# 100 small fill-ups and two large ones first, one product on VectorE, one group of transposes moved forward

## The chip, the cores and the metric

The kernel runs on one core of one Trainium2 chip. The metric is the device time of one execution in microseconds (us). The kernel before took 466.82 us, the median of three runs (466.12 to 467.25).

The engines are TensorE (PE in the profile; its weight loads are a stream of their own, PEld), VectorE (DVE), ScalarE (ACT), GpSimd (POOL) and SyncE (SP), which here issues the transfers.

## The reference

A gated linear attention over four batches, eight heads, 768 steps and a head size of 48, and behind it a two-layer block on 3072 tokens.

```python
f = 1.0 / (1.0 + np.exp(-f_logit))
for t in range(S):
    state = f[:, :, t, :, None] * state + np.einsum('bhd,bhe->bhde', k[:, :, t], v[:, :, t])
    y[:, :, t] = np.einsum('bhd,bhde->bhe', q[:, :, t], state)
x = y.transpose(0, 2, 1, 3).reshape(B * S, H * D)
h = x @ w_in                                  # 384 -> 2048
g = h * np.clip(h + 3.0, 0.0, 6.0) / 6.0
return g @ w_out                              # 2048 -> 384
```

## The kernel before

The attention is cut into 24 units, one for each batch and chunk of 128 steps; unit `i` has batch `i % 4` and chunk `i // 4`, so units 0 to 3 are the first chunks of the four batches. The two-layer block is cut into six groups of 512 tokens (the four units of one chunk) by 16 slices of 128 hidden columns.

The order of all work is written out by hand in `ORDER` (L55): a list of tokens such as `kv.1.2`, which means step `kv` of unit 1 with PSUM bank 2. The tokens are issued one after the other, and each engine executes its own instructions strictly in the order of the list (the loop at the end of `gla_moe` chains them). So a token's place relative to another one matters only where both have instructions on one engine. `ON_POOL` (L48) lists the elementwise steps that go to GpSimd instead of VectorE; the function `engine` looks them up.

What the early tokens do, with the lines under which the profile shows them:

- `load`, `loadq`, `loadv`, `ld`, `hole`: transfers on SP (gates, q and k, v, a slice of the weights in float32, and rows of the attention's output that are moved between partitions).
- `gate` (ScalarE, L321): sigmoid. `back` (VectorE, L327) and `fwd` (L347): scans over the gates, backwards and forwards. `rend` (VectorE, L343 and L344): the ends of the decay and their reciprocals.
- `kmul` (L340) and `qmul` (L353): k and q times the decay. `kmul.1` stands in `ON_POOL` and runs on GpSimd; the other early ones run on VectorE.
- `tk` (TensorE, L411): four transposes of k. `ktok` (ScalarE, L418): their copy out of PSUM.
- `kv` (TensorE, L430): the state's update, 24 matmuls in a unit of the first chunk; every float32 matmul is two passes in the profile, so 48. `carry0`, `carry1` (ScalarE, L443 and L450, in the first chunk): its copies out of PSUM.
- `att` (TensorE, L392) and `mask` (VectorE, L399): the scores inside a chunk. `qs` (TensorE, L461) and `av` (L478): the two parts of the output, "values" in what follows.
- `xh` (ScalarE, L497), `xs` (TensorE, L501), `xl` (ScalarE, L508): the output split into a high and a low half-precision part.
- `z` (ScalarE, L243), `cy` (ScalarE, L252), `mid` (VectorE, L256), `dif` (L263), `top` (L267), `high` (ScalarE, L272), `lowi` (L275): the rounding and splitting of a slice of weights.
- `mm1a`, `relua`, `ga`, `mm2a` and their kin: the two-layer block.
- `warm.n` (L804): a fill-up. It multiplies the zero tile `blank` into the bank `idle`, which nothing reads, in matmuls of up to four times 128 columns: `warm.16` is four matmuls of 512 columns, `warm.3` one of 384. Being float32, each is two passes. TensorE executes them in its order like any other matmul.

At the start VectorE clears `blank`, and TensorE begins with `warm.16`. `tk.0` waits for `kmul.0`, `ktok.0` for `tk.0`, `kv.0` for `ktok.0`, `att.0` for `carry0.0` (it takes over the PSUM bank) and `qmul.0`, `mask.0` for `att.0`, and `av.0` for `mask.0` and `qs.0`.

## Time and profile before

| | us |
|---|---|
| median of three runs | 466.82 |
| lowest and highest run | 466.12, 467.25 |
| the profiled execution | 468.3 |
| its span, first to last instruction | 466.6 |

The profile's page gives the busy time of each engine with its share of the span and its number of instructions, the chain of work that ended last with its shares, and the groups of instructions. Times in the trace are counted from the start of the span. A row of the timeline reads: start, duration in us, engine, line, operation, output and input tiles, shape, number of instructions merged, and in brackets the idle time of the engine before it with what ended it ("issue" where the profile names nothing). A row of the windows view reads: the stretch, its length, then busy time and number of instructions of PE, PEld, DVE, ACT and POOL, the granted TensorE clock as a share of full speed, the busy share of the DMA engines, and GB/s. In the DMA view, a line gives a queue with its kind, packets, MB and share of 16 engines. Some matmul records can be missing from a trace, a few per cent.

### The profile page before, as it was taken

How to read it: one execution, taken by the hardware profiler on the slowest of the kernel's cores; microseconds unless marked ns; L12 is line 12 of the kernel's file. 1: busy time of each engine (PE TensorE's matmuls, PEld its weight loads, DVE VectorE, ACT ScalarE, POOL GpSimd, SP SyncE). 2: the span in 40 equal slices, each digit the busy share in tenths (PEclk: the TensorE clock that was granted, in tenths of full speed). 3: DMA queues.
4: the chain of work that ended last, by engine and by line, in shares of the span. 5: the costliest groups of instructions: out<-in, count | busy, mean ns of one | idle time of the engine just before them, and what ended most of it. 6: DMA issues, size and time to landing. Idle time of an engine off the chain costs nothing.

```text
span 466.6 us, 11487 instructions
## 1 busy us (share of the span) xinstructions
PE 459.2 (98%) x4963; PEld 247.5 (53%) x4963; DVE 300.1 (64%) x508; ACT 205.1 (44%) x344; POOL 79.3 (17%) x85
## 2 busy tenths in 40 slices
PE   8899999999999999999999999999999999999996
PEld 4678855544445644554545444665644444555543
DVE  6889999968697748746443596879752312423554
ACT  3577777764353243435142541344433423233332
POOL 3000311132012320322210051241200231000000
PEclk9799999999999999999999999999999999999999
DMA  8569647520430150510212120522020000010002
GB/s 301 188 249 353 249 181 249 198 84 0 135 108 1 51 206 0 153 46 0 87 31 91 42 94 1 196 90 76 4 80 0 1 0 6 24 45 3 0 1 68
DMA packets 25396, 43.09 MB, mean 92 GB/s; under 512 B 2560, under 2 KB 17152, under 8 KB 25344
## 3 DMA queue, kind: packets, MB, share of 16 engines
q1 hardware_dynamic: 23744, 41.56, 26.0%
q8 instruction: 39, 0.64, 0.6%
q10 hardware_dynamic: 1600, 0.79, 0.6%
q14 instruction: 13, 0.11, 0.1%
HBM read 36.43 MB, written 4.72 MB: 88 GB/s over the span
## 4 chain that ended last, share of the span: by engine, by line
PE 97%; DVE 1%; ACT 1%; issue 1%; DVEq 0%
PE o L582 35%; PE pair L536 26%; PE single L536 13%; PE pair L461 3%; PE o L621 3%; PE pair L478 3%; PE pair L392 3%; PE pair L430 2%; PE idle L804 2%; PE o L593 2%; PE pair L636 1%; PE single L636 1%; PE single L603 1%; PE pair L603 1%; PE pair L411 1%; PE single L411 1%
## 5 line engine op out<-in xcount | busy, mean ns | idle before, releaser
L582 PE MATMUL o<-gg,weight 128*128 128x512 f16 x744 | 170.2, 379 | 0.0
L536 PEld LDWEIGHTS <-weight 128*128 128x128 f16 x819 | 78.7, 98 | 93.6 <-issue 0.8
L536 PE MATMUL pair<-xts,weight 128*128 128x512 f16 x549 | 125.9, 379 | 0.0
L582 PEld LDWEIGHTS <-weight 128*128 128x128 f16 x744 | 72.0, 98 | 82.4 <-issue 0.7
L555 ACT ACTIVATE gg<-tg 128x512 f16<-128x512 f32 x88 | 54.5, 627 | 62.5 <-DVE tg L550 56.1
L550 DVE SCALAR_TENSOR_TENSOR tg<-tg,pair 128x512 f32<-128x512 f32 x61 | 41.3, 682 | 62.7 <-ACT tg L546 62.6
L546 ACT ACTIVATE tg<-pair,half 128x512 f32<-128x512 f32 x61 | 41.5, 683 | 66.6 <-PE pair L536 64.8
L565 POOL TENSOR_TENSOR gg<-tg,gg 128x512 f16<-128x512 f32 x33 | 40.1, 1225 | 167.1 <-ACT gg L555 148.1
L536 PE MATMUL single<-xts,weight 128*128 128x512 f16 x270 | 63.3, 379 | 0.0
L550 DVE SCALAR_TENSOR_TENSOR tg<-tg,single 128x512 f32<-128x512 f32 x30 | 20.5, 683 | 33.2 <-ACT tg L546 33.2
L546 ACT ACTIVATE tg<-single,half 128x512 f32<-128x512 f32 x30 | 20.6, 686 | 45.0 <-PE single L536 43.3
L347 DVE TENSOR_TENSOR_SCAN suffix<-gates,rend 112x516 f32<-112x516 f32 x24 | 30.6, 1276 | 4.3 <-POOL qkf L340 3.7
L327 DVE TENSOR_TENSOR_SCAN suffix<-gates,unit 112x516 f32<-112x516 f32 x24 | 29.9, 1248 | 5.1 <-ACT gates L321 5.0
L565 DVE TENSOR_TENSOR gg<-tg,gg 128x512 f16<-128x512 f32 x39 | 27.0, 702 | 8.4 <-ACT gg L555 8.2
L497 ACT ACTIVATE xts<-pair 112x512 f16<-112x512 f32 x24 | 14.3, 595 | 30.2 <-PE pair L478 17.8
L340 POOL TENSOR_TENSOR qkf<-qkf,suffix 112x512 f32<-112x512 f32 x13 | 17.0, 1309 | 47.1 <-DVE suffix L327 43.4
L399 DVE TENSOR_TENSOR a<-pair,causal 128x512 f32<-128x512 f32 x24 | 16.4, 684 | 13.0 <-PE pair L392 10.2
L510 DVE SCALAR_TENSOR_TENSOR xts<-pair,xts 112x512 f16<-112x512 f32 x20 | 13.6, 682 | 8.5 <-ACT xts L497 8.4
L321 ACT ACTIVATE gates<-gates 112x512 f32<-112x512 f32 x24 | 14.9, 623 | 5.2 <-DMA gates<-fg 5.2
L430 PE MATMUL pair<-v,ktok 64*48 64x48 f32 (+1 forms) x768 | 15.8, 214 | 1.3 <-issue 1.3
L478 PE MATMUL pair<-a,v 64*48 64x64 f32 (+1 forms) x768 | 16.2, 222 | 0.6 <-DVE a L399 0.2
L392 PE MATMUL pair<-qkf 48*64 48x64 f32 x768 | 16.4, 224 | 0.2 <-ACT state L450 0.2
(99 smaller groups left out, 447.5 us busy)
## 6 DMA issues: line engine op xcount, KB each, us to landing
qkf<-qk SPq DMA_DIRECT2D x24, 512.0 KB, 5.0
raw<-w SPq DMA_DIRECT2D x16, 768.0 KB, 5.6
gates<-fg SPq DMA_DIRECT2D x24, 258.5 KB, 3.7
v<-v SPq DMA_DIRECT2D x24, 200.0 KB, 3.3
outT<-os SPq DMA_DIRECT2D x10, 256.0 KB, 2.7
outT<-os SPq DMA_DIRECT2D x10, 128.0 KB, 1.9
xts<-xts SPq DMA_DIRECT2D x48, 24.0 KB, 1.9
outT<-os ACTq DMA_DIRECT2D x2, 256.0 KB, 2.6
```

The source lines that it names most:

```text
L327: nc.vector.tensor_tensor_scan(flat(sf)[:, ::-1], gt[:, 1:][:, ::-1], flat(unit)[:, ::-1], 0.0, op0=ALU.mult, op1=ALU.add,)
L340: engine("kmul", i).tensor_tensor(parts_of(t, 1), parts_of(t, 1), split(sf[:, :, 1:C + 1]), op=ALU.mult)
L347: nc.vector.tensor_tensor_scan(flat(sf), gt[:, :NP * (C + 1)], flat(rend), 0.0, op0=ALU.mult, op1=ALU.add,)
L392: nc.tensor.matmul(d["at"][HC * odd:HC * (odd + 1), e, 2 * n + c], t[rs, 1, n, c, odd], t[rs, 0, n, c, odd], start=True, stop=True,)
L430: nc.tensor.matmul(d["kv"][r:r + m, odd, c, n], d["ktok"][rs, 2 * n + part, r:r + m], heads_of(vt[rs], part, n, e)[:, :D], start=(odd, e) ...
L478: nc.tensor.matmul(d["y"][to:to + m, odd, n, cs], heads_of(vt[rs], c, n, e)[:, :m], d["a"][rs, 2 * n + c, e], start=False, stop=True, skip ...
L536: nc.tensor.matmul(h, win[:, f, a, k * 128:(k + 1) * 128], g["xt"][:, k, :g["n"] // C, b], start=i == 0, stop=i == 3 * KT - 1,)
L546: nc.scalar.activation(d["t"], d["h"], AF.Relu, bias=half, scale=RISE)
L550: nc.vector.scalar_tensor_tensor(d["t"], d["t"], TOP, d["h"], op0=ALU.min, op1=ALU.mult)
L555: nc.scalar.activation(d["gg"][:, 0], d["t"], AF.Copy)
L565: engine("gl", int(g["name"]) * NF + f).tensor_tensor(d["gg"][:, 1], d["t"], d["gg"][:, 0], op=ALU.subtract)
L582: nc.tensor.matmul(g["o"][m], wout[:, f, a, m * 128:(m + 1) * 128], g[f]["gg"][:, b], start=f == 0 and i == 0, stop=f == NF - 1 and i == 2 ...
```

## The change

Four things are edited.

1. `warm.16` at the start becomes `brief.100 warm.8`. `brief.100` is a new token: 100 matmuls of a bf16 zero tile `small` with 32 weight columns and 32 moving columns, into a corner of `idle`. `warm.8` is two matmuls of 512 columns. The tile `small` is cleared on VectorE ahead of `blank`.
2. `kmul.1` leaves `ON_POOL`, so it runs on VectorE, and its token moves to a place ahead of `rend.1`.
3. `tk.1.4 ktok.1` moves ahead of `av.0 xh.0`.
4. The fill-up `warm.1` ahead of `av.0` is dropped.

```diff
 ON_POOL = """
-kmul.1 decay.4 kmul.6 lowi.5 kmul.7 decay.7 lowi.7 kmul.8 gl.9 decay.8 gl.11 qmul.8 gl.12 lowo.0 low.15 lowo.3 gl.19
+decay.4 kmul.6 lowi.5 kmul.7 decay.7 lowi.7 kmul.8 gl.9 decay.8 gl.11 qmul.8 gl.12 lowo.0 low.15 lowo.3 gl.19
...
 ORDER = """
-load.0 gate.0 back.0 loadq.0 loadv.0 rend.0 kmul.0 load.1 fwd.0 gate.1 back.1 warm.16 tk.0.3 ktok.0 warm.4 kv.0.0
-carry0.0 load.2 qmul.0 warm.1 att.0.0 loadq.1 ld.0 rend.1 qs.0.2 mask.0 gate.2 warm.1 av.0 xh.0 kmul.1 tk.1.4 ktok.1
+load.0 gate.0 back.0 loadq.0 loadv.0 rend.0 kmul.0 load.1 fwd.0 gate.1 back.1 brief.100 warm.8 tk.0.3 ktok.0 warm.4 kv.0.0
+carry0.0 load.2 qmul.0 warm.1 att.0.0 loadq.1 ld.0 kmul.1 rend.1 qs.0.2 mask.0 gate.2 tk.1.4 ktok.1 av.0 xh.0
 carry1.0 fwd.1 qmul.1 warm.3 att.1.0 xs.0 loadv.1 back.2 mask.1 rend.2 cy.0 load.3 kv.1.2 z.0 mid.0 loadq.2 gate.3
...
+    small = const.tile([128, 64], BF16, name="small")
+    nc.vector.memset(small, 0.0)
     blank = const.tile([128, 128], F32, name="blank")
     nc.vector.memset(blank, 0.0)
...
-        if op == "warm":
+        if op == "brief":
+            for _ in range(i):
+                nc.tensor.matmul(idle[:32, :32], small[:, :32], small[:, :32], start=True, stop=True)
+        elif op == "warm":
             for at in range(0, i, 4):
```

The early stretch of `ORDER` that the prediction follows, behind these lines, is the same in both:

```python
carry1.0 fwd.1 qmul.1 warm.3 att.1.0 xs.0 loadv.1 back.2 mask.1 rend.2 cy.0 load.3 kv.1.2 z.0 mid.0 loadq.2 gate.3
back.3 ld.1 carry0.1 warm.1 qs.1.0 dif.0 kmul.2 top.0 fwd.2 xl.0 carry1.1 loadq.3 av.1 hole.0 tk.2.4 rend.3 xh.1 xs.1
xl.1 z.1 qmul.2 warm.3 att.2.2 kmul.3 cy.1 mid.1 fwd.3 ktok.2 loadv.2 high.0 warm.4 kv.2.0 carry0.2 tk.3.4 ktok.3
```

## The prediction

> **What bounds the kernel now.** I read the page's busy times and the chain of work that ended last, then the list of what each engine waited for, split at 30 us, then the timeline, the DMA view and the one-microsecond windows of the first 30 us.

> ```profile
> PE 459.2 (98%) x4963; PEld 247.5 (53%) x4963; DVE 300.1 (64%) x508; ACT 205.1 (44%) x344; POOL 79.3 (17%) x85
> q8 instruction: 39, 0.64, 0.6%
> PE 97%; DVE 1%; ACT 1%; issue 1%; DVEq 0%
> ```

> TensorE is the bound: 97% of the chain. Asked for 30 to 467 us, the waits view lists no wait of TensorE at all. So a microsecond gained or lost before 30 us moves the end by about a microsecond: every transfer and every other engine behind it waits for a buffer or a result that moves along. The change lies wholly before 30 us.

> ```profile
> PE pair L430 <- issue: 1.3, 1, 1.3
> DVE raw L256 <- ACT top L252: 2.0, 1, 2.0
> 14.70 0.78 PE L430 MATMUL pair<-v,ktok 64*64 64x48 f32 x34
> 16.75 0.66 PE L430 MATMUL pair<-v,ktok 64*48 64x48 f32 x14 [1.27 <-issue]
> 0.00:15.47 15.47, 13.88 (x220) 7.93 (x221) 11.63 (x23) 7.22 (x13) 4.23 (x17) 1.00 0.88 328
> q1 hardware_dynamic: 1556, 4.52, 87.4%
> q8 instruction: 1, 0.02, 4.6%
> q8 instruction: 1, 0.02, 3.8%
> ```

> The one large hole of TensorE is the 1.27 us in the middle of `kv.1`: 34 of its 48 matmuls run, then nothing, and no semaphore is named. The last three lines are the DMA view of 0 to 14 us, where the data queue is the only one, and the instruction queue's line of 14.0 to 15.4 and of 17.5 to 19.0 us: one packet each, and none between. The page has 39 such packets for 2 x 4963 TensorE instructions, 254 each. So I read the hole as a lack of instructions: 220 + 221 = 441 were there at the start, the next block came in near 15 us, and TensorE went on at 16.75. One block earlier is instruction 441 - 254 = 187; TensorE passes it inside `att.0`, near 10.4 us. If the request goes out there, 6.3 us pass until use, while the data queue keeps the DMA engines full.

> ```profile
> 16.00:17.00 1.00, 0.25 (x12) 0.25 (x12) 1.00 (x2) 0.00 (x0) 0.00 (x0) 0.90 0.08 33
> 18.00:19.00 1.00, 0.91 (x21) 0.67 (x24) 1.00 (x3) 0.50 (x2) 0.00 (x0) 0.50 0.00 0
> 23.00:24.00 1.00, 1.00 (x29) 0.82 (x22) 0.39 (x2) 1.00 (x3) 0.00 (x0) 0.69 0.14 38
> ```

> The third number from the right is the granted clock, the next the DMA share. The clock is 1.00 in the stretch to 15.47, then 0.90, 0.50 and 0.69: halved from about 16.8 to 23.6 us, right after the hole.

> **The change part by part.** *The fill-ups.* Before, `warm.16` is four instructions, eight passes, and `tk.0` stands behind them.

> ```profile
> 1.13 6.38 PE L804 MATMUL idle<-blank 128*128 128x512 f32 x8 [1.13 <-DVE blank L208]
> 7.34 0.55 PE L411 MATMUL pair<-ident,qkf 112*128 112x112 f32 x4
> 7.73 1.04 PE L804 MATMUL idle<-blank 128*128 128x512 f32 x2
> 22.58 1.13 PE L392 MATMUL pair<-qkf 48*64 48x64 f32 x32
> ```

> The first eight passes start some 0.8 us apart, the pair at 7.73 us needs 0.52 each: the first run at half clock. Four of them go, 3.4 us, and 100 small matmuls come. No row shows one of 32 by 32. The nearest is the last one above: at half clock, 32 matmuls of 64 columns in two-pass f32, on four parts of the array in turn, take 1.13 us, 0.035 each. On one part that is at most 0.14 a matmul, and a quarter of that, 0.035, for half the columns in one pass of bf16. The lower end is 0.027, by the last row less its run-out of some 0.25 us ((1.13 - 0.25) / 32). The upper end is 0.054, twice that, if no weight load hides behind the matmul before it; but loads (247.5 us) do run beside matmuls (459.2 us) in a span of 466.6. I take 0.035: 3.5 us, for 3.4 removed. The ends are 2.7 and 5.4 us, that is `tk.0` 0.7 us earlier or 2.0 later. Earlier brings at most 0.35 us, since `ktok.0` stands behind `gate.1` on ScalarE. The memset of the small tile costs under 0.1 us on VectorE ahead of `blank`, at a time when VectorE then waits for the first gates anyway.

> *Where the instruction blocks fall.* The small ones add 100 pairs, four passes fewer take 4, the fill-up `warm.1` ahead of `av.0` takes 2: 94 pairs, 188 instructions more. Instruction 187 now falls among the small ones, near 4.3 us, and instruction 442 in the first third of `av.0`, near 11.8 us. The same 6.3 us from request to use gives 10.6 us: in time by 1.2. The block behind that starts at 441 + 254 = 695, in `av.1`; it is requested at 11.8, the data queue is nearly empty by 16 us (share 0.08), and I let it be usable at 16.75 as before, when `av.1` is just due. So both waits are about zero, and 1.27 goes.

> *`kmul.1` on VectorE.*

> ```profile
> 8.97 1.48 POOL L340 TENSOR_TENSOR qkf<-qkf,suffix 112x512 f32<-112x512 f32 x1 [5.24 <-DVE suffix L327]
> 9.32 1.16 DVE L343 TENSOR_SCALAR ends<-suffix 112x4 f32<-112x4 f32 x1
> 15.15 0.16 DVE L343 TENSOR_SCALAR ends<-suffix 112x4 f32<-112x4 f32 x1
> 10.89 0.69 DVE L399 TENSOR_TENSOR a<-pair,causal 128x512 f32<-128x512 f32 x1 [0.20 <-PE pair L392]
> 17.43 0.68 DVE L340 TENSOR_TENSOR qkf<-qkf,suffix 112x512 f32<-112x512 f32 x1
> ```

> GpSimd needs 1.48 us, and the `ends` operation beside it takes 1.16 instead of 0.16. After, the product takes 0.68 on VectorE (last row) and `ends` 0.16 again: 0.32 us less ahead of `mask.0`. That buys nothing: `mask.0` already waits 0.20 for `att.0`, and its wait grows to about 0.5. On GpSimd, `decay.4` is next, a later unit's. SP's queue keeps its order; no DMA is added or moved.

> *`tk.1`, `ktok.1` in front of `av.0`, `xh.0`.*

> ```profile
> 10.58 0.41 PE L461 MATMUL pair<-qkf,middle 48*64 48x64 f32 x16
> 11.64 0.69 PE L478 MATMUL pair<-a,v 64*64 64x64 f32 x32 [0.23 <-DVE a L399]
> 12.76 0.69 DVE L353 TENSOR_TENSOR qkf<-qkf,suffix 112x512 f32<-112x512 f32 x1
> 12.90 0.54 ACT L418 ACTIVATE ktok<-single 128x448 f32<-128x448 f32 x1
> 13.34 0.33 ACT L450 ACTIVATE state<-pair 112x192 f32<-112x192 f32 x1
> 13.71 0.69 PE L392 MATMUL pair<-qkf 48*64 48x64 f32 x32 [0.19 <-ACT state L450]
> 14.34 0.43 PE L501 MATMUL pair<-xts,less 112*112 112x256 f16 x2
> 17.68 0.59 ACT L508 ACTIVATE xts<-pair 112x512 f16<-112x512 f32 x1
> ```

> `tk.1` (0.55, as `tk.0`) takes the place of the removed fill-up, about 11.0 to 11.55 us, while `mask.0` runs until 11.58. Behind it wait `av.0`, then `xh.0` and `carry1.0` on ScalarE. `kmul.1` is done by 10.1, so the new wait is empty; were it late, `av.0` would be late by as much. `ktok.1` (0.54) moves out from between `xh.0` and `carry1.0`, so the latter starts near 13.0 instead of 13.34. `att.1` (13.71) then waits for `qmul.1`, which VectorE ends at 13.45, and comes 0.1 us earlier. VectorE, busy without a gap to 21.61, takes no notice: counted as 0.

> *What follows when the hole is gone.*

> ```profile
> 15.18 0.61 ACT L321 ACTIVATE gates<-gates 112x512 f32<-112x512 f32 x1
> 18.85 1.13 PE L478 MATMUL pair<-a,v 64*64 64x64 f32 x32
> 20.92 0.69 DVE L340 TENSOR_TENSOR qkf<-qkf,suffix 112x512 f32<-112x512 f32 x1
> 21.91 0.88 ACT L243 ACTIVATE whole<-raw 128x768 int32<-128x768 uint32 x1
> 22.69 0.89 ACT L252 ACTIVATE top<-raw 128x768 int16<-128x768 int16 x1
> 23.61 0.36 DVE L256 TENSOR_SCALAR raw<-top 128x768 int16<-128x768 int16 x1 [2.00 <-ACT top L252]
> 24.70 0.91 PE L430 MATMUL pair<-v,ktok 64*64 64x48 f32 x48
> ```

> `kv.1` runs through: 14.70 + 0.91 = 15.6. ScalarE is free from `gate.3` at 15.79, so `carry0.1` (0.33) ends at 16.15, `qs.1` (0.41) at 16.6, `av.1` (0.69 at full clock) at 17.35 instead of 19.98. Now `tk.2` is late next: it waits for VectorE's `kmul.2` (17.43 + 0.68 = 18.11) and ends at 18.8; `xs.1` (0.43) 19.2, `xl.1` (0.59) 19.8, then `z.1` and `cy.1` on ScalarE, 0.88 and 0.89: 21.6. VectorE comes free at 21.61. So `mid.1` starts at 21.65 instead of 23.61: **2.0 us**. On TensorE `kv.2` follows the fill-up behind `att.2`: VectorE's `qmul.2`, just ahead of the row at 20.92, is done by 21.0; `att.2` 0.69 and `warm.4` 1.04 later it is 22.7 instead of 24.70, 2.0 too. The sum is 0 + 0 + 0 + 2.0.

> The profiled execution took 468.3 us with a span of 466.6; the median of the three timed runs is 466.82. I take the 2.0 from the median: **464.8 us**. With the fill-ups at their short end it is 464.4.

> [...] The clock fell behind a hole of 1.27 us, the longest TensorE had. [...]

> **The rivals.** *The clock stays halved (or comes up late).* For it: TensorE would still have gaps near 17.4 to 18.2 and 20 to 21 us; and in 18 to 19 us it was busy 0.91 at half clock without being released, so small matmuls seem to count for less than the large passes that they replace. Against: up to 15.47 the clock is full over the same kind of work. Price: at half clock a group takes 1.13 / 0.69 = 1.64 times as long. `tk.2` 0.9, `xs.1` 0.7, `warm.3` 1.3, `att.2` 1.13, `warm.4` 1.7: from 18.2 this puts `kv.2` near 23.95, a gain of 0.75: 466.1. A first release that comes later, near 10 us, ends alike: `kv.0` would run 1.5 us later, VectorE too, of 2.0 to gain: 466.3.

> *The change doesn't do what it says: the hole is no matter of instruction blocks.* The waits view only says "issue". Then 94 more pairs move nothing, and what is left is the 0.1 us at `att.1`: 466.7. [...]

> *Slower: the hole moves forward.* If a block gets through only as the first loads drain, and not a fixed time behind its request, then it is usable at 16.75 whenever it was asked for, and TensorE stops in `av.0` from 11.8 to 16.75. Behind it come 0.45 for the rest of `av.0`, `xh.0` 0.6, `carry1.0` 0.33, `att.1` 1.13 at a clock that has fallen, and hand-overs of some 0.2: `mask.1` starts near 19.5 instead of 14.5. VectorE is 5 us late, and the 2.0 of slack at `mid.1` take up two. Price 3.0: 469.8. It turns from gain to loss where the block is usable after some 14 us. For it: the one fetch seen while data moved came in just before the data ran out. Against: it did come in while data still moved.

> **How the numbers follow.** Forecast 464.8, chance 0.45, own range 464.3 to 465.6. Clock rival 0.25 (465.6 to 466.6). No effect 0.12 (466.7). Slower 0.18 (467.8 to 469.8, where a partial stop is likelier than the full one). A measurement of this kernel tells about 0.2%, 0.9 us, from no change: below 465.9 is faster. That is the forecast and a quarter of the clock rival, 0.51; same 0.31; slower 0.18. For 8 in 10 the range runs from 464.0 (fill-ups at 0.027, and 0.4 more if TensorE's chain gains over VectorE's) to 467.8, which leaves out the slower case and a little below.

> **What would show it.** Right: no issue wait in L430; an instruction packet before 10 us; VectorE's wait at L256 gone or under 0.3; the clock at 1.00 from 16 to 24 us; L343 at 0.16 each. Wrong: 100 small matmuls that last over 4.5 us; an issue wait at L478 near 12 us; a clock of 0.50 after 7 us. It would also be wrong if the waits view after 30 us showed new waits of TensorE, from blocks that now end in other groups.

## The result, and the profile after

| | before | after |
|---|---|---|
| median of six runs, us | 466.41 | 471.13 |
| lowest and highest, us | 466.12, 467.25 | 469.60, 475.22 |
| the profiled execution and its span, us | 468.3, 466.6 | 469.6, 467.8 |

The change makes the kernel slower: the ratio of after to before is 1.0109, with a 95% interval of 1.0069 to 1.0149. The forecast was 464.8 us and its range ended at 467.8. The lines of the changed kernel are numbered 2 to 5 higher: `av` is L480, `kv` L432, `att` L394, `kmul` L342, `mid` L258.

First the page of after: its span, TensorE's busy time, the instruction queue and the chain of work that ended last. Then the lines of TensorE and of `mid` in the list of waits, from 0 to 30 us, and below the mark the one line of TensorE from 30 to 468 us.

```profile
span 467.8 us, 11673 instructions
...
PE 456.7 (98%) x5057; PEld 247.1 (53%) x5057; DVE 299.5 (64%) x510; ACT 205.2 (44%) x344; POOL 77.8 (17%) x84
...
q8 instruction: 40, 0.66, 0.6%
...
PE 94%; DMA 1%; issue 1%; DVE 1%; ACT 1%; SPq 0%; DVEq 0%
```

```profile
PE pair L480 <- issue: 1.3, 1, 1.3
...
DVE raw L258 <- ACT top L254: 0.8, 1, 0.8
...
PE pair L432 <- issue: 0.5, 1, 0.5
...
PE pair L480 <- issue: 1.0, 1, 1.0
```

Before, the hole in `kv.1` was TensorE's only wait of this kind. Now there are three, in `av.1`, `kv.3` and `av.15`; the last lies near 298 us, in a stretch that the change did not edit. The instruction queue has 40 packets instead of 39. TensorE's busy time is not higher (456.7 us; 459.2 in the profile that the prediction read, 456.3 in a second profile of before that is told of below), so the loss is not work.

Next, rows of the timeline of the first 32 us of after.

```profile
1.03 2.85 PE L805 MATMUL idle<-small 128*32 128x32 bf16 x100 [1.03 <-DVE small L208]
3.81 3.37 PE L809 MATMUL idle<-blank 128*128 128x512 f32 x4
...
10.06 0.69 DVE L342 TENSOR_TENSOR qkf<-qkf,suffix 112x512 f32<-112x512 f32 x1 [0.49 <-DMA qkf<-qk]
10.67 0.16 DVE L345 TENSOR_SCALAR ends<-suffix 112x4 f32<-112x4 f32 x1
...
10.96 0.68 DVE L401 TENSOR_TENSOR a<-pair,causal 128x512 f32<-128x512 f32 x1
...
16.58 0.33 PE L480 MATMUL pair<-a,v 64*64 64x64 f32 x2
18.20 0.68 PE L480 MATMUL pair<-a,v 64*64 64x64 f32 x30 [1.30 <-issue]
...
22.29 0.36 DVE L258 TENSOR_SCALAR raw<-top 128x768 int16<-128x768 int16 x1 [0.82 <-ACT top L254]
...
22.74 0.91 PE L432 MATMUL pair<-v,ktok 64*64 64x48 f32 x48
27.24 0.74 PE L432 MATMUL pair<-v,ktok 64*64 64x48 f32 x38
28.48 0.38 PE L432 MATMUL pair<-v,ktok 64*48 64x48 f32 x10 [0.51 <-issue]
```

The edited steps do what was forecast of them, and `kv.2` starts at 22.74 us, as forecast (22.7); `mid.1` starts at 22.29, not at 21.65. But two groups are broken, `av.1` (2 matmuls, a stop, 30 more) and `kv.3` (38 and 10), with no semaphore named.

The third hole, in the timeline of after near 298 us:

```profile
296.66 0.63 PE L480 MATMUL pair<-a,v 64*48 64x64 f32 x26
298.27 0.32 PE L480 MATMUL pair<-a,v 64*48 64x64 f32 x4 [0.99 <-issue]
```

The trace also says when a block comes. Below is the DMA view of after in four short stretches: 15.8 to 16.0 us, 26.0 to 26.2, 295.8 to 296.0 and 463.2 to 463.4. Each holds one packet of the instruction queue (columns: packets, MB, share).

```profile
q8 instruction: 1, 0.02, 32.9%
...
q8 instruction: 1, 0.02, 30.6%
...
q8 instruction: 1, 0.02, 32.3%
...
q8 instruction: 1, 0.02, 39.2%
```

In the trace these packets start at 15.84, 26.05, 295.87 and 463.24 us. TensorE goes on at 18.20, 28.48 and 298.27: 2.4 us behind the packet each time. In these cases the packet itself follows the moment when TensorE passed the end of the block before. The table has that moment for the holes of after and, for `kv.3`, of later runs.

| hole | block before ends | packet starts | TensorE goes on | from end to use |
|---|---|---|---|---|
| before, `kv.1` | 10.52 | 14.31 | 16.75 | 6.2 |
| after, `av.1` | 11.82 | 15.84 | 18.20 | 6.4 |
| after, `kv.3` | 24.12 | 26.05 | 28.48 | 4.4 |
| after, `av.15` | 294.76 | 295.87 | 298.27 | 3.5 |
| after, second profile, `kv.3` | 23.96 | 26.78 | 29.20 | 5.2 |
| 94 small ones, `kv.3` | 24.61 | 29.45 | 31.92 | 7.3 |

So in these rows one block is fetched while the one before it runs, and from the end of one block to the start of the block after the next it is 3.5 to 7.3 us. The holes came where TensorE ran through 256 records faster than that. `att`, `kv`, `qs` and `av` of one unit do: in after the block ahead of `kv.3` lasted 3.6 us (24.12 to 27.76). A short block alone is not enough: in before the one that ends near 202 us lasted 2.7 us, without a stop. And the request is not tied to the record that is being executed: in stretches of long matmuls the packet starts up to 4.3 us before TensorE passes the end of its block (all forty of after counted). What releases it is not shown.

**The end.** The DMA view from 460 us to the end shows how long the last two stores take to land (last number, a median of the two), in after:

```profile
outT<-os ACTq DMA_DIRECT2D x2, 128.0 KB, 3.3
```

and in the kernel before, in a second profile that is told of below:

```profile
outT<-os ACTq DMA_DIRECT2D x2, 128.0 KB, 1.9
```

The fortieth packet of instructions starts at 463.24 us, 0.3 us behind the issue of the last store, and nothing of what it brings is needed. From the start of the last matmuls to the end of the span after takes some 1.3 us longer (below).

### The profile page after: what moved, and what is told of

Read it like the earlier page. It is cut to its first block, busy times and chain, and to the rows that moved or that the text cites. A ratio compares the mean times of both kernels' runs of the same rounds, so it can differ in the third digit from the quotient of the medians.

```text
span 467.8 us, 11673 instructions
## 1 busy us (share of the span) xinstructions
PE 456.7 (98%) x5057; PEld 247.1 (53%) x5057; DVE 299.5 (64%) x510; ACT 205.2 (44%) x344; POOL 77.8 (17%) x84
## 4 chain that ended last, share of the span: by engine, by line
PE 94%; DMA 1%; issue 1%; DVE 1%; ACT 1%; SPq 0%; DVEq 0%
PE o L584 35%; PE pair L538 26%; PE single L538 13%; PE pair L463 3%; PE o L623 3%; PE pair L480 3%; PE pair L394 2%; PE pair L432 2%; PE o L595 2%; DMA qkf<-qk 1%; PE pair L638 1%; PE single L638 1%; PE single L605 1%; PE pair L605 1%; PE pair L413 1%
## 5 line engine op out<-in xcount | busy, mean ns | idle before, releaser
L342 POOL TENSOR_TENSOR qkf<-qkf,suffix 112x512 f32<-112x512 f32 x12 | 15.5, 1295 | 42.5 <-DVE suffix L329 38.8
L480 PE MATMUL pair<-a,v 64*48 64x64 f32 (+1 forms) x768 | 16.4, 218 | 2.9 <-issue 2.3
L394 PE MATMUL pair<-qkf 48*64 48x64 f32 x768 | 16.0, 220 | 0.7 <-DVE qkf L355 0.7
L269 DVE SCALAR_TENSOR_TENSOR whole<-top,whole 128x768 int16<-128x768 int16 x16 | 16.4, 1025 | 0.1
```

Of the source, the lines that this page charges most:

```text
L269: nc.vector.scalar_tensor_tensor(upper, conv[f]["y"], 8.0, upper, op0=ALU.mult, op1=ALU.add)
L394: nc.tensor.matmul(d["at"][HC * odd:HC * (odd + 1), e, 2 * n + c], t[rs, 1, n, c, odd], t[rs, 0, n, c, odd], start=True, stop=True,)
L480: nc.tensor.matmul(d["y"][to:to + m, odd, n, cs], heads_of(vt[rs], c, n, e)[:, :m], d["a"][rs, 2 * n + c, e], start=False, stop=True, skip ...
```

## The experiments

Two readings stood against each other. **Block ends:** each part of the loss comes from the count of TensorE instructions ahead of a dense group, not from the steps that were edited. **The edits:** the reordered steps, or the fill-ups themselves, cost the time. Ratios are to the kernel before, run on the same chip at the same time (median 466.38 to 466.72), with 95% intervals.

### The kernel before once more

No edit.

> The kernel before, once more, for a second trace of it. Theory B2: most of its timed runs have a mean clock of 0.998 or 0.999 and a span near 464.4 us, where the execution that the prediction was made from had 0.993 and 466.6. If this execution is one of the common ones, the clock is at 1.00 from 16 to 24 us although the hole in kv.1 (1.2 to 1.3 us) is there, kv.2 starts near 22.5 instead of 24.70, and the last matmul comes 2.2 us earlier: the 2.0 us that were forecast are then the price of that clock and not of the hole. Rival: the hole is absent in these runs.

It took 466.12 us with a span of 464.4, while the profile that the prediction read had 468.3 and 466.6. Rows of its timeline, and then its windows view from 17 to 23 us:

```profile
14.45 0.78 PE L430 MATMUL pair<-v,ktok 64*64 64x48 f32 x34
16.31 0.43 PE L430 MATMUL pair<-v,ktok 64*48 64x48 f32 x14 [1.08 <-issue]
21.84 0.36 DVE L256 TENSOR_SCALAR raw<-top 128x768 int16<-128x768 int16 x1 [0.43 <-ACT top L252]
22.54 0.91 PE L430 MATMUL pair<-v,ktok 64*64 64x48 f32 x48
```

```profile
17.00:23.00 6.00, 5.06 (x126) 3.03 (x126) 5.53 (x10) 4.80 (x9) 0.00 (x0) 1.00 0.38 104
```

The hole is there, 1.08 us long, but the clock (third number from the right) stays at 1.00, and `kv.2` starts at 22.54 us, not 24.70. VectorE's wait at L256 is 0.43, not 2.00. The hole by itself costs little: VectorE is busy 5.53 of these 6 us, and bounds them. So the 2.0 us were the price of the halved clock in one execution. A median of 466.82 with a distance of 1.7 between time and span has a span near 465, so the typical run did not contain them.

### The fill-ups alone

```diff
-... back.1 warm.16 tk.0.3 ...
+... back.1 brief.98 warm.8 tk.0.3 ...
```

`warm.1` and the old order stay, so the count of instructions is the changed kernel's.

> The kernel before with the fill-ups alone changed: 98 small ones and two large ones in place of four large ones, so that TensorE has exactly the 188 instructions more of the changed kernel; the order of the product and the transposes as before. Theory B (instruction blocks): in the two traces the holes named issue lie at instruction records 449 (before), 705, 1217 and 7361 (after), all 449 plus a multiple of 256, so it is the count of instructions in front that places them. Then this kernel has the after kernel's holes: about 1.3 us in av.1 near 17 us, about 0.5 in kv.3 near 28 us, about 1.0 in av.15 near 298 us, an instruction packet during the last store and an end about 1 us later; its time is that of the changed kernel within 1 us, 470 to 472. Rival O (the product on VectorE and the earlier transposes cost the time): no slower than before, 464.5 to 466.5.

It took 472.87 us (471.84 to 473.88, ratio 1.0129, 1.0087 to 1.0172). The waits, 0 to 30 us and, below the mark, from 30 us on; then the windows view from 19 to 26 us:

```profile
PE pair L480 <- issue: 1.3, 1, 1.3
...
PE pair L480 <- issue: 1.4, 1, 1.4
PE pair L432 <- issue: 0.9, 1, 0.9
```

```profile
19.00:26.00 7.00, 6.83 (x90) 3.83 (x89) 5.99 (x12) 3.74 (x7) 0.00 (x0) 0.52 0.62 193
```

The same three holes, at the same three records, without any reordering: the whole loss comes with the fill-ups. It is a little larger than after's, because here the clock also fell behind the hole in `av.1` (0.52 from 19 to 26 us).

### The order alone

```diff
-kmul.1 decay.4 ...
+decay.4 ...
-... ld.0 rend.1 qs.0.2 mask.0 gate.2 warm.1 av.0 xh.0 kmul.1 tk.1.4 ktok.1
+... ld.0 kmul.1 rend.1 qs.0.2 mask.0 gate.2 tk.1.4 ktok.1 warm.1 av.0 xh.0
```

> The other half alone: the product of unit 1 on VectorE and its transposes and their copy in front, with the four large fill-ups and the one-pass fill-up kept, so that TensorE has the instructions of before in number. Theory B: the hole in kv.1 stays (1.2 to 1.3 us), none after 30 us, time within 0.2% of before, 465.7 to 467.0. Rival O: 469 to 471.

It took 467.29 us (465.76 to 468.51, ratio 1.0003, 0.9980 to 1.0026). Its only issue waits are 0.9 us at L430, near 16 us at the end of the same block, 449, and 0.4 at L411. The second is no block end: it lies at 6.6 us ahead of `tk.0`, which starts 0.1 us behind the end of VectorE's `kmul.0`. So the product on VectorE and the earlier transposes cost nothing and bring nothing, as the prediction counted them.

### 118 and 94 small fill-ups

```diff
-brief.100 warm.8
+brief.118 warm.6
```

> The changed kernel with 118 small fill-ups and 512 plus 256 columns of large ones: 36 instructions more in front. Theory B, with the times from one block's end to the next one's use read off the trace of before: the hole at the start of qs.1 is about 0.7 us instead of 1.3 in av.1, that in av.15 and the others after 30 us go (the nearest block has 0.7 us to spare), so the last matmul ends 1.5 to 2.5 us earlier than in the changed kernel and the time is 468 to 469.5, or 467 if the instruction packet at the end lies before the last store. Rival C (the small fill-ups let the clock fall, whatever the blocks): still 470 to 472.

469.01 us (467.26 to 470.79, ratio 1.0051, 1.0022 to 1.0080). Every block now ends 36 records earlier in the program. The holes go with them: 0.9 us at L463, and 1.4 in `kv.3`, now behind 20 matmuls instead of 38. (A wait of 0.4 at L413 is again the one ahead of `tk.0`, at 6.7 us.) The one at 298 us shrinks to 0.6, where none was expected, and the last packet comes at 458.4 us, ahead of the stores.

```diff
-brief.100 warm.8
+brief.94 warm.8
```

> The changed kernel with 94 small fill-ups instead of 100. Its last TensorE instruction is then record 10175, two short of the block's end at 10177 (449 plus 38 times 256), where the changed kernel runs ten past it. Theory B: 39 instruction packets instead of 40, none during the last store, and the stretch from the last matmul to the end is that of before (4.3 us instead of 5.6), 1 us less; a hole of 0.5 to 1.0 us stays near 298 us, now at the transposes behind av.15. Time 469.5 to 470.5. Rival: the end is 1 us longer for another reason than the packet, and stays so.

475.07 us (472.72 to 477.25, ratio 1.0170, 1.0112 to 1.0229). The expectation was missed twice: the fortieth packet is still there, at 469.3 us, though the trace ends two records short of 10177 (other packets start ahead of the end of their block too, as said above), and `kv.3` lost far more than foreseen. `av.0` stopped too, for 1.0 us until 12.70: its packet came at 10.46, where after has it at 6.24. Its line in the waits from 30 us on, and windows behind it:

```profile
PE pair L432 <- issue: 3.5, 1, 3.5
```

```profile
29.00:31.00 2.00, 0.00 (x0) 0.00 (x0) 1.93 (x4) 0.00 (x0) 0.00 (x0) 1.00 0.71 279
31.00:38.00 7.00, 5.99 (x67) 4.73 (x68) 1.68 (x2) 2.96 (x7) 0.51 (x1) 0.54 0.06 16
```

TensorE stands still for 3.5 us, and then runs at about half clock for 7. The packet was 4.8 us late behind the block's end (24.61 to 29.45) while data kept the DMA engines at a share of 0.96. Twelve instructions fewer than in after made the kernel 4 us slower: which block end meets what decides, not the number of fill-ups.

### The blocks moved in front of `kv.2`

```diff
-high.0 warm.4 kv.2.0
+high.0 brief.48 kv.2.0
```

The changed kernel with 92 more TensorE instructions, which do nothing useful.

> The changed kernel with 48 small fill-ups in place of the one-matmul, 512-column fill-up ahead of kv.2: 92 TensorE instructions more from there on, so the holes before that stay and all later block ends move. Theory B: the hole in av.1 stays (1.3 us), that in kv.3 shrinks from 0.5 and more to 0.3 or less, as its block is asked for 92 instructions earlier; none at av.15; the instruction packet comes 4 us before the last store is issued and the stretch from the last matmul to the end is 4.3 us. Time 467.0 to 468.5, 3 to 4 us less than the changed kernel. Rival (the start, or the clock, costs the time): still 470 to 472.

467.71 us (466.48 to 469.14, ratio 1.0020, 1.0004 to 1.0037), 3.4 us less than after. The hole in `av.1` stays (1.3 us; a wait of 0.8 at L413 is the one ahead of `tk.0`, at 6.6 us), TensorE has no issue wait behind 30 us, and the last packet comes at 448.8 us. Adding instructions took away two holes and the collision at the end, and left the first hole, which the second profile of before shows to be nearly free. This is the clearest evidence for block ends.

### Before, with 94 more pairs late

```diff
-nc.tensor.matmul(h, ..., start=i == 0, stop=i == 3 * KT - 1)
+parts = [(0, 2), (2, 4)] if 0 < i <= split else [(0, 4)]
+for lo, hi in parts:
+    nc.tensor.matmul(h[:, lo * C:hi * C], ..., start=i == 0, stop=i == 3 * KT - 1, skip_group_check=True)
```

In the kernel before, 94 matmuls of `mm1` of 512 columns, between about 90 and 120 us, are done as two of 256: 188 instructions more, as in after, with nothing edited ahead of them.

> The kernel before with nothing changed before 90 us; in the first layer's products of slices 9 to 20 of the hidden columns, 94 matmuls of 512 columns are issued as two of 256, which gives 94 pairs of TensorE instructions more by 150 us at next to no work. Theory B: the same hole in av.15 as in the changed kernel (about 1.0 to 1.4 us) and the same packet at the end (1.1 to 1.7 us): 468.5 to 469.5, plus up to 0.9 us for the split itself. Rival (holes come from what is done, not from where the blocks end): no hole near 298 us, an end of 4.3 us, 466 to 467.3.

469.38 us (467.32 to 469.96, ratio 1.0044, 1.0023 to 1.0064). Its one issue wait behind 30 us:

```profile
PE pair L479 <- issue: 1.4, 1, 1.4
```

That is the third hole, in `av.15` at record 7361, made in the old kernel by the count alone. Its last packet comes at 463.2 us and its end is late as in after. The splits themselves cost some 0.2 us: ScalarE's rows lie 0.21 us behind those of the second profile of before at 64 us, ahead of the splits, and 0.45 at 161. The first hole is 0.45 us long here instead of 1.08, and `kv.2` starts no earlier (22.75).

### After, with 18 more pairs late

The same edit in the changed kernel with 18 splits near 95 us, so that all places behind it move on by 36 records.

> The changed kernel with 18 such splits near 95 us, 36 instructions more from there on. Theory B: holes in av.1 and kv.3 as in the changed kernel, none after 100 us, an end of 4.3 us instead of 5.6: 2.1 to 2.6 us less than the changed kernel, 468.5 to 469. The difference to e6 is then the price of the hole in kv.3. Rival: 470 to 472.

469.92 us (467.23 to 472.00, ratio 1.0049, 1.0021 to 1.0076). The hole at record 7361 falls to 0.4 us, the last packet (462.0 us) is ahead of the last stores, and the end is no longer late. The median is above what was expected. `kv.3`, which lies ahead of the edit, lost 2.3 us in this profile, with half clock behind it (0.51 from 30 to 37 us); the profile is of the slowest of the seven runs (472.00), so how much of the median that explains is open.

### After once more

No edit. The question was where the spread of 469.6 to 475.2 us comes from.

> The changed kernel once more, nothing edited. Its six timed runs spread over 469.6 to 475.2 us, and the one profiled was the fastest; no profile shows a slow one. Theory: the spread sits in kv.3, where the block of instructions from record 1217 on competes with data transfers. Then a profile of 470.5 us or more shows a hole of over 1 us in kv.3 (0.5 in the profile at hand), and where it is over 2 us a granted clock of 0.5 for some 7 us behind it; the waits behind 30 us stay one of 1.0 us in av.15, and the end stays at 5.0 to 6.0 us from the last matmul. Rival: the spread is elsewhere (the clock at some other place, or the last store); then the hole in kv.3 stays at 0.5 to 0.8 and the clock at 1.00 around it.

471.60 and 472.85 us. The profile is of the first. Its timeline, and its windows view from 30.0 to 33.5 us:

```profile
27.07 0.74 PE L432 MATMUL pair<-v,ktok 64*64 64x48 f32 x38
29.20 0.38 PE L432 MATMUL pair<-v,ktok 64*48 64x48 f32 x10 [1.40 <-issue]
...
300.40 0.60 PE L413 MATMUL single<-ident,qkf 112*128 112x112 f32 x4
...
463.23 1.15 PE L638 MATMUL single<-gg,weight 128*128 128x256 f16 x9
```

```profile
30.00:33.50 3.50, 3.43 (x57) 2.61 (x58) 2.10 (x4) 2.02 (x4) 0.51 (x1) 0.51 0.13 42
```

The hole in `kv.3` is 1.40 us, and the clock is halved for 3.4 us behind it: as expected, but for the half clock, which came already behind 1.4 us and not only behind 2, and for the stop in `av.15`, which is 0.7 us and not 1.0. With the second profile of before as the yardstick the loss can be read place by place. Its rows:

```profile
27.04 0.85 PE L430 MATMUL pair<-v,ktok 64*64 64x48 f32 x48
...
295.81 0.65 PE L478 MATMUL pair<-a,v 64*48 64x64 f32 x30
296.39 0.60 PE L411 MATMUL single<-ident,qkf 112*128 112x112 f32 x4
...
459.21 1.15 PE L636 MATMUL single<-gg,weight 128*128 128x256 f16 x9
```

and those of after, where they have not been shown:

```profile
298.51 0.60 PE L413 MATMUL single<-ident,qkf 112*128 112x112 f32 x4
...
461.34 1.15 PE L638 MATMUL single<-gg,weight 128*128 128x256 f16 x9
```

| start of | before, second profile | after, first | after, second |
|---|---|---|---|
| `kv.2` | 22.54 | 22.74 (+0.20) | 22.57 (+0.03) |
| end of `kv.3` | 27.89 | 28.86 (+0.97) | 29.58 (+1.69) |
| `av.15`, main part | 295.81 | 296.66 (+0.85) | 298.82 (+3.01) |
| transposes behind `av.15` | 296.39 | 298.51 (+2.12) | 300.40 (+4.01) |
| last group of matmuls | 459.21 | 461.34 (+2.13) | 463.23 (+4.02) |
| end of the span | 464.4 | 467.8 (+3.4) | 469.8 (+5.4) |

`kv.3` costs 0.8 to 1.7 us, and in the second profile the clock behind it another 1.3; `av.15` costs 1.0 to 1.3; the last store 1.3 to 1.4.

### Blocks moved at the start too

```diff
-brief.100 warm.8 ... warm.3 att.2.2 ... warm.4 kv.2.0
+brief.66 warm.10 ... brief.30 att.2.2 ... brief.52 kv.2.0
```

This was to get rid of the hole in `av.1` as well, and to beat the kernel before if that hole counted.

> The changed kernel with brief.66 warm.10 for brief.100 warm.8, brief.30 for the warm.3 ahead of att.2 and brief.52 for the warm.4 ahead of kv.2. Record 705 falls 64 records later, from av.1 to tk.2, where TensorE waits for kmul.2 anyway; all records behind kv.2 stand within a few of where the run with the blocks moved at kv.2 had them (467.71). Theory that a block end costs only where TensorE has nothing else to wait for: the issue wait at L480 goes, no issue wait of over 0.3 us behind 30 us, end from last matmul 4.3 to 4.5 us. VectorE bounds the stretch to mid.1, so at most 0.4 us come of it: 466.3 to 467.6, which doesn't beat the kernel before by more than 0.2%. Rival, that the hole in av.1 held everything up by its full 1.3 us: 465.0 to 465.8, faster than both.

468.33 us (467.48 to 472.09, ratio 1.0039, 1.0019 to 1.0059). The hole in `av.1` is gone, no issue wait is over 0.4 us in one piece, and yet neither number was met. The timeline and the windows view say why:

```profile
18.56 0.92 PE L805 MATMUL idle<-small 128*32 128x32 bf16 x30
21.33 1.55 PE L805 MATMUL idle<-small 128*32 128x32 bf16 x52
```

```profile
17.00:21.00 4.00, 2.10 (x66) 1.68 (x58) 3.97 (x8) 2.93 (x5) 0.00 (x0) 1.00 0.48 134
21.00:25.00 4.00, 4.00 (x132) 3.72 (x124) 4.00 (x8) 1.33 (x3) 0.00 (x0) 0.57 0.81 262
```

TensorE was busy 2.10 of 4 us up to 21, with waits for VectorE in place of the hole and small matmuls in place of the large fill-up, and then the clock fell to about half for 3.4 us. Whether the clock fell for the small matmuls or for the waits was not tried apart. No version that I ran beats the kernel before.

### Data out of the way

```diff
-... ktok.4 loadv.4 ld.3 cy.3
-z.3 hole.2 mid.2 ...
+... ktok.4 hole.2 loadv.4 ld.3 cy.3
+z.3 mid.2 ...
```

This is the kernel with 94 small ones, with 0.97 MB of transfers requested later on SP's queue.

> The kernel with 94 small fill-ups (475.07 us, hole of 3.5 us in kv.3, half clock behind it), with hole.2 moved ahead of loadv.4, ld.3, cy.3 on SP's queue, so that 0.97 MB of data are requested only after xl.3, near 31 us, in place of 24 us. Theory that the packet of instructions of record 1217 is held up by the data: what is still on the queues then is 1.7 MB from 22.5 us, at some 0.4 MB per us until about 27, so the packet starts by 27.3 and TensorE goes on by 29.7: a hole of at most 1.4 us, no half clock, 471.0 to 473.0 us. Rival, that the delay has another cause (the request itself is late): a hole of 3 to 3.7 us as before, 474.5 to 476.5.

472.83 us (472.11 to 474.60, ratio 1.0139, 1.0108 to 1.0171), inside the expected band. `kv.3` is whole again:

```profile
29.64 1.14 PE L432 MATMUL pair<-v,ktok 64*64 64x48 f32 x48
```

But the test is not clean. In this profile the clock had already fallen at 19.6 us, so the block's end was passed at 26.64, not 24.61, when less data was left; the packet came 1.4 us behind it, at 28.04, as the DMA share fell from 0.81 to 0.24. That data holds the packet up agrees with this, but is not proved apart. A busy DMA alone does not do it: from 295 to 296 us in after the share was 1.02, and the packet came 1.1 us behind the block's end.

### The last packet moved ahead of the stores

The split of `mm1` once more, in the changed kernel, 40 matmuls behind 390 us: everything up to there stays as it is.

> The changed kernel with 40 matmuls of 512 columns of slices 80 to 84 of mm1, behind 390 us, split into two of 256 columns each: the same products, 80 TensorE instructions more. The holes of kv.3 and av.15 lie ahead of it and stay (0.5 to 2 us and 1.0 us). Record 10177, with which the 40th packet of instructions was asked for at 462.0 us, is passed some 9 us earlier, so that the packet no longer lies on the last store. Theory that it delays that store: last packet before 458 us, from the last matmul to the end of the span 4.3 to 4.5 us instead of 5.6, median 1.0 to 1.4 us below the changed kernel: 469.6 to 470.3. Rival, that the longer end belongs to the late run of the kernel itself (its stores are slower whatever the packet does): 5.5 to 5.8 us from the last matmul, median 471 to 472.

470.01 us (468.57 to 471.93, ratio 1.0069, 1.0048 to 1.0089), 1.1 us less than after; the two intervals overlap, so the medians alone do not settle it. The last packet starts at 454.5 us, 4.0 us ahead of record 10177, so that record is not what asks for it; and the two last stores land in 1.9 us again:

```profile
outT<-os ACTq DMA_DIRECT2D x2, 128.0 KB, 1.9
```

All fourteen profiles say the same: from the start of the last group of matmuls to the end of the span it is 5.2 to 5.3 us in the eight whose last packet starts ahead of that group, and 6.3 to 7.0 in the six whose packet starts 1.9 us behind its start. The useless fortieth packet on the last store cost the rest of the end, 1.3 us in the table above. The rival, a late run whose stores are slow whatever the packet does, falls.

## Why the prediction was wrong

**What held.** The bound behind 25 us: TensorE, so that the losses in `kv.3` and `av.15` reach the end. (Ahead of that it did not hold: VectorE bounds that stretch, and the holes in `kv.1` and `av.1` are nearly free.) The blocks: 254 counted, 256 found. The first new request: its packet came at 6.24 us, and `av.0` ran without a stop. The order: nothing for `kmul.1` and the transposes, 0.16 us each for `ends`, `mask.0` at 10.96 instead of 10.89.

**Mis-sized without effect.** The 100 small matmuls took 2.85 us, 0.0285 each and not 0.035. `kmul.1` waited 0.49 us for unit 1's q and k, a wait that the prediction did not look for; it ended at 10.75 instead of 10.1 and still in front of `mask.0`. The clock row of 1.00 to 15.47 us holds only from 6.55 us on, where the trace's clock record begins.

**First step that failed: 2.0 us taken from the median.** The end of the working, `kv.2` at 22.7, came out at 22.74, but not because the hole was gone: it had moved to `av.1`. `kv.2` hangs on VectorE's `qmul.2`, which ended at 20.86 all the same, so the number is no proof of the step. `mid.1`, the other end, came at 22.29 instead of 21.65, and its wait was 0.82 us where under 0.3 was the sign of being right. Above all, the execution that was profiled was 1.5 us above the median, and the clock at half from 16.8 to 23.6 us was what set it apart. The second profile of before has the hole without the halving, and `kv.2` at 22.54. The gain was already in the number from which it was taken. The prediction said that the span and the median differ, and did not ask which stretch made the difference.

**Second: "usable at 16.75 as before, when `av.1` is just due".** For the first block the prediction used 6.3 us from request to use; for the second, requested at 11.8, it took another rule. Its own 6.3 gives 18.1. Measured: 18.20, a hole of 1.30 us. That puts back the hole of before, in another place and nearly as free as it was.

**Third, and this is what made the kernel slower: "every other engine behind it waits for a buffer or a result that moves along".** That holds for buffers and results. It does not hold for block ends, which stay at fixed counts while the program moves under them. The prediction listed new waits after 30 us from blocks that now end in other groups as a sign against itself, but gave them neither a price nor a chance. Its trace had what it takes to find the places: the count of the added records, the 6.3 us, and the dense groups of 256. A price was harder to get, as short blocks ran without a stop in before. `kv.3`, `av.15` and the last store add up to 3.3 us in the first profile of after and 4.0 in the second by the table, where the clock behind `kv.3` adds another 1.3.

**The rivals.** The slower one had the right kind of cause, a block that comes late behind the data of the first loads, at the wrong place: `av.0`, which was served (with 94 small ones it did stop, for 1.0 us); the late block came in `av.1`, nearly free, and then in `kv.3`. The one in which the hole is no matter of instruction blocks falls: the runs show one block fetched ahead, and holes of 0.4 to 3.5 us at block ends. The clock rival did not show in after's first 24 us (1.00 from 6.6 us on in its first profile), but a halved clock did cost 1.3 us behind `kv.3` in its second profile.

## What to carry to other kernels

Before a gain is subtracted from a median, look at what sets the profiled execution apart from it; a stretch of lower clock in one profile is not there to be won. Where an edit changes the number of instructions of the busiest engine, even of useless ones, count the records: each block end behind it moves. Here one that landed in a dense group (256 records in 2.3 us in `av.15` and 3.6 in `kv.3`), in a stretch full of transfers (share 0.97 around `kv.3`) or on the last store cost 0.8 to 1.7 us in the profiles of after, and nearly nothing in `kv.1` and `av.1`, where VectorE bounded the stretch. Padding with 48 cheap instructions at a place that had slack moved them away again (3.4 us), but it has to be looked at as a whole, as each shift brings other places up.

## What the hardware showed unexpectedly

- The holes at block ends stand at records 449 + 256 k exactly, the sequencer's rows counted in (449 in before; 705, 1217 and 7361 in after). Not every wait that the list calls issue is one (`tk.0` above). From the start of the packet to the next instruction it is 2.2 to 2.5 us when TensorE waits for it, at 14 us as at 296, with one exception: 3.4 us with 118 small ones, in `av.15`, where the packet itself took 1.9 us (the median is 1.04 in before and 1.05 in after).
- The clock's answer to a hole varied. Behind 1.08 us (before, second profile) and 1.30 (after) it stayed at 1.00, behind 1.3 (the fill-ups alone), 1.27 (before, first) and 1.40 (after, second) it was halved. In the clock record of before's first profile it is full for 10.24 us, from 6.55 to 16.79, and then halved for 6.83. By the windows, the half-clock stretch lasted 3.4 us behind `kv.3` in the second profile of after (0.51 from 30.0 to 33.5 us) and 6.9 with the fill-ups alone (0.52 from 19 to 26, 0.92 from 26 to 27). What sets these lengths is not shown.
- The small matmuls were no faster at full clock: 30 of them took 0.92 us in the run with the blocks moved at the start (granted clock 1.00 from 17 to 21 us), 0.031 each, against 0.0285 at the beginning of after (100 in 2.85 us), ahead of the trace's clock record, which begins at 6.64 us.
